# Pooled attention and a tanh-shrink MLP on one core: loads ahead of stores, key placement on ScalarE, product seven in halves, values of two blocks a unit later

## The chip, the core and the metric

The kernel runs on one core of a Trainium2 chip. The metric is the device time in microseconds (us) of one execution; lower is better. Five engines work side by side and wait for each other through semaphores: TensorE (PE, with its weight loads shown apart as PEld), VectorE (DVE), ScalarE (ACT), GpSimd (POOL) and SyncE (SP), which here only issues DMAs. Each engine takes its instructions in the order of the program.

## What is computed

The reference, cut to what matters (batch 8, 8 heads, 576 positions, 64 per head; `w_in` is 512 x 2048, `w_out` 2048 x 512):

```python
k_p = k.reshape(B, H, 72, 8, D).mean(axis=3)
v_p = v.reshape(B, H, 72, 8, D).mean(axis=3)
attn = softmax(q @ k_p.T / sqrt(D))          # with the row maximum taken off
x = (attn @ v_p) as 4608 tokens of 512
h = x @ w_in
g = h - tanh(h)
out = g @ w_out
```

## The kernel before

**Groups.** The 4608 tokens are worked in nine groups of 512. Groups 0 to 7 are the first 512 positions of a batch element; group 8 holds the last 64 positions of all eight, the tails. Two batch elements make one tail unit. While group g runs its MLP, the attention of batch element nb = g + 1 is computed between its matmuls, and keys, values and queries of later elements are loaded.

**First half of a group.** `h_mms` (L445) runs 64 matmuls of 512 columns, four for each of 16 slices of the hidden layer. After every second slice `h_act` takes the tanh on ScalarE (L458) and subtracts it on VectorE into `gT` (L459). All 64 read `xT`, so they need all four blocks of the group's `x`.

**Second half, groups 3 to 8 (`SEVEN`).** The product with `w_out` is done as seven products of quarter matrices, with sums of quarters made beforehand. Their order is 4, 2, 7, 1, 6, 5, 3. Each has two column halves b = 0 and 1 of eight matmuls of 256 columns (L591), so there are 14 units u = 0 to 13, called 4b0, 4b1, 2b0 and so on here. Products 4, 7, 1, 6, 5, 3 add into one PSUM bank for each b, and `evacuate` copies the state of the bank out after each (L606, L608, L611 on ScalarE, L618 on VectorE for product 3). `g_sum` (L573) makes the left-hand sums: S3 in two halves (`g_sum(3, 0, 4)` after slice 13 and `g_sum(3, 4, 8)` after slice 15, stored in the memory of `q_raw[1]`), read by product 7; S2, read by product 6; two on GpSimd, read by product 5; and `g_sum(4)`, after unit 8, read by product 3. `finish_11` and `finish_22` on GpSimd complete the two output halves, and `store_half` stores each (512 KB).

**Attention between the matmuls.** Four blocks of 128 rows, and a tail unit when the element closes a pair (nb = 5 and 7 among these groups). For each: scores on PE (`s`, L311; reads `qT` and `KB`), row maximum and subtraction on VectorE (L323, L326), exp on ScalarE into E (`e`, L362), a DMA transpose of E into ET (`t`, L371), values on PE (`a`, L398), normalisation on VectorE (L419, L420), and a DMA transpose of x into `xT` (`x`, L428). `PLAN7` says at which slice (negative numbers) or after which unit each step stands. Its second half before the change:

```python
0: [("e", 3), ("t", 1)],
3: [("a", 0, P67)],
5: [("a", 1, P45), ("x", 0)],
6: [("a", 2, P67)],
7: [("a", 3, P45), ("x", 1)],
9: [("sb", 4, P45)],
11: [("e", 4), ("t", 2)],
```

P45 and P67 are pairs of PSUM banks. The values and the x transpose of a tail unit are carried into the next group (`carry`, after units 9 and 10).

**Keys, values, queries.** `pool_k` (L214, L217, L220) and `pool_v` (L229 to L256) pool on GpSimd. The pooled keys `kd` are transposed by DMA into `kT` (`k_turn_dma`, L272), and `k_place_kT` (L266) copies them by two instructions of 64 partitions x 288 into `KB`, before on GpSimd. Queries are cast on ScalarE (L280) and transposed by DMA (`q_turn_dma`, L286). Tail queries are loaded (`tail_pieces`, L176), cast on GpSimd (`tail_cast`, L184) and transposed by DMA (`turn_tail`, L187).

**SP's queue.** SP issues every DMA of groups 3 to 6, one after the other in program order, and waits at an entry whose data aren't ready. Before the change, the second half of a group that has later elements to load (groups 3 to 5) issues in this order: values of element nb + 1; transpose of E (blocks 2 and 3, unit 0); transpose of q; first transpose of x (unit 5); second transpose of x, then of kT, then the tail loads when nb is even (unit 7); transpose of the tail's E (unit 11, when there is a tail); store of half 1 (unit 11); keys and queries of a later element (`load_for`, unit 13); store of half 0 (unit 13).

Of the kernel before, what the change touches and what calls it, by code (L numbers as in the profile page):

```python
# [31 lines left out]
NQ = NHID // 2  # L32
HC = DM // 2
SEVEN = (3, 4, 5, 6, 7, 8)
# [4 lines left out]
def kernel(  # L39
# [83 lines left out]
    def raw_of(b):  # L123
        return 1 if b == 1 else 0
# [30 lines left out]
    def k_pieces(b):  # L155
        return row_pieces(k_rows, k_raw, b)
# [13 lines left out]
    def run(pieces, n=16):  # L170
        for _ in range(min(n, len(pieces))):
            pieces.pop(0)()

    def tail_pieces(i, eng=None):
        return [
            lambda s=s: (eng or nc.sync).dma_start(  # L176
                out=tl_raw[64 * s : 64 * s + 64, :, :],
                in_=q[2 * i + s, :, QA:S, :].rearrange("h p d -> p h d"),
            )
            for s in range(2)  # L180
        ]

    def tail_cast(i):
        nc.gpsimd.tensor_copy(out=tl_bf[i % 2][:, :, :], in_=tl_raw[:, :, :])  # L184
# [25 lines left out]
    def pool_k(b, eng, t0=0, t1=NT):  # L210
        r = k_raw[raw_of(b)].rearrange("p t (j d) -> p t j d", d=D)[:, t0:t1, :, :]
        kd = kds[b % 2][:, t0:t1, :, :]
        n = t1 - t0
        eng.tensor_tensor(  # L214
            out=r[:, :, 0:4, :], in0=r[:, :, 0:4, :], in1=r[:, :, 4:8, :], op=ALU.add
        )
        eng.tensor_tensor(  # L217
            out=r[:, :, 0:2, :], in0=r[:, :, 0:2, :], in1=r[:, :, 2:4, :], op=ALU.add
        )
        return eng.tensor_tensor(  # L220
            out=kd,
            in0=r[:, :, 0:1, :].to_broadcast([128, n, 2, D]),
            in1=r[:, :, 1:2, :].to_broadcast([128, n, 2, D]),
            op=ALU.add,
        )
# [50 lines left out]
    def k_place_kT(b, eng):  # L276
        k_place(b, kTs[b % 2].rearrange("p t c -> p (t c)")[:, 0:NK], (eng, eng))
# [297 lines left out]
    XB, YB = 2, (0, 1)  # L575
    PRODUCTS = ("4", "2", "7", "1", "6", "5", "3")

    def product(n, b):

        A, a0, B_ = {  # L580
            "1": (gT[:, HI, C1], 0, w2b[:, HI, C1]),
            "2": (gT[:, LO, C1], 0, w2b[:, LO, C1]),
            "3": (gT[:, LO, C1], 0, w2b[:, LO, C2]),
            "4": (gT[:, LO, C2], 0, T4),
            "5": (gT[:, HI, C2], 0, T1),
            "6": (S2, 0, T2),
            "7": (S3, 0, T3),
        }[n]
        ps = PS[:, XB, HC * b : HC * b + HC] if n == "2" else PS[:, YB[b], 0:HC]
        for i in range(NQ):  # L590
            nc.tensor.matmul(  # L591
                ps,
                lhsT=A[:, i, 128 * b : 128 * b + 128],
                rhs=B_[:, i, :],
                start=(n in "24" and i == 0),
                stop=(i == NQ - 1),
                skip_group_check=True,
            )

    def evacuate(n, b, plain=False):  # L600
        ps = PS[:, YB[b], 0:HC]
        if n == "2":
            if b == 1:
                nc.scalar.copy(out=p2, in_=PS[:, XB, :].rearrange("p (b c) -> p b c", b=2))
        elif n in "47":
            nc.scalar.copy(out={"4": n0, "7": n1}[n][:, b, :], in_=ps)  # L606
        elif n == "6":
            nc.scalar.copy(out=o_hs[1][:, b, C1], in_=ps)  # L608
        elif plain and n in "15":
            dst = o_hs[0][:, b, C1] if n == "1" else o_hs[1][:, b, C2]  # L610
            nc.scalar.copy(out=dst, in_=ps)  # L611
        else:
            dst, sub = {
                "1": (o_hs[0][:, b, C1], n1),
                "5": (o_hs[1][:, b, C2], n0),
                "3": (o_hs[0][:, b, C2], n1),
            }[n]
            nc.vector.tensor_sub(out=dst, in0=ps, in1=sub[:, b, :])  # L618
# [7 lines left out]
    def finish_22(eng):  # L626
        o = o_hs[1][:, :, C2]
        eng.tensor_tensor(out=o, in0=o, in1=n0, op=ALU.subtract)

    def store_half(g, hf):  # L630
        blk = out[g * S : g * S + QA, :].rearrange("(p j) m -> p j m", j=R)
        nc.sync.dma_start(out=blk[:, 2 * hf : 2 * hf + 2, :], in_=o_hs[hf][:, :, :])
# [18 lines left out]
    ve, se, ge = nc.vector.tensor_copy, nc.scalar.copy, nc.gpsimd.tensor_copy  # L651
# [167 lines left out]
    def load_for(g):  # L819


        r = []
        if g + 2 < B:
            if g in SEVEN:
                r += k_pieces(g + 2) + q_pieces(g + 2)
            else:
                r += (v_pieces(g + 1) if g == 2 else []) + q_pieces(g + 2) + k_pieces(g + 2)
        run(r)
# [28 lines left out]
    for u in range(16):  # L857
# [50 lines left out]
    P23, P45, P67 = (2, 3), (4, 5), (6, 7)  # L908
# [8 lines left out]
        0: [("e", 3), ("t", 1)],  # L917
        3: [("a", 0, P67)],
        5: [("a", 1, P45), ("x", 0)],
        6: [("a", 2, P67)],  # L920
        7: [("a", 3, P45), ("x", 1)],
        9: [("sb", 4, P45)],
        11: [("e", 4), ("t", 2)],
    }
    late, carry = [], []

    def tail_values(i):
        av_mms(slot_tl, av_tail(i), P67)
# [6 lines left out]
    for g in range(1, NG):  # L935
        nb = g + 1 if g + 1 < B else None
        more = nb is not None and nb + 1 < B

        tail = {2: 0, 3: 1, 5: 2, 7: 3}.get(nb)
# [33 lines left out]
            pool_v(nb, nc.gpsimd)  # L973
        if more and g in SEVEN:
            pool_k(nb + 1, nc.gpsimd)
        shs = {}

        def seven_more(u):
            if u == 0:
                q_turn_dma(nb + 1)  # L980
            if u == 7:
                k_turn_dma(nb + 1)
                if nb % 2 == 0:
                    run(tail_pieces(nb // 2))
            if u == 13:
                k_place_kT(nb + 1, ge)
                if nb % 2 == 0:
                    tail_cast(nb // 2)
                load_for(g + 1)

        def step(kind, n, bk=None):
            if kind == "t2":
                e_turn_dma(units[2][2], n, n + 1)
                return
            if kind == "t":
                e_turn_dma(units[2 * n][2], 0, 2 if n < 2 else 1)
                if tail and n == 0:
                    turn_tail(tail)
                return
            if kind == "x":  # L1000
                x_turn_dma(xs[n], *((nb, 2 * n, 2) if n < 2 else (B, tail, 1)))
                return
            s, a, sl = units[n]
            if kind == "s" and bk:
                s_mms(s, bk)
                ng = s_max(bk)
                late.append(lambda: s_exp_heads(bk, ng, sl))
            elif kind in ("s", "sb"):
                bk = bk or PAIRS[s_pairs[n]]
                s_mms(s, bk)  # L1010
                shs[n] = s_shift(bk)
            elif kind == "e":
                s_exp(shs[n], sl)
            else:
                bk = bk or PAIRS[a_pairs[n]]
                av_mms(sl, a, bk)
                normalise(bk, xs[n // 2][:, n % 2, :, :, :])
# [23 lines left out]
            run(v_next)  # L1041
        for u in range(14 if g in SEVEN else 0):
            n, b = PRODUCTS[u // 2], u % 2
            product(n, b)
            evacuate(n, b, nb is not None)
            for it in plan.get(u, ()):
                step(*it)
                run_late()
            if nb is not None and u in (9, 10) and carry:
                carry.pop(0)()  # L1050
            if more:
                seven_more(u)
            if nb is not None and u == 2:
                dep = g_sum(2, 0, NQ)
                after([g_sum(1, 0, 4, nc.gpsimd), g_sum(1, 4, NQ, nc.gpsimd)], dep)
            if u == (3 if nb is None else 8):
                g_sum(4, 0, NQ)
            if g == NG - 1:
                if n == "1" and b:
                    finish_11(nc.vector)  # L1060
                    store_part(0, C1, 0, 2)
                elif n == "6" and b:
                    store_part(1, C1, 0, 2)
                elif n == "5" and b:
                    store_part(1, C2, 0, 2, (nc.sync, nc.scalar))
                elif n == "3":
                    store_part(0, C2, b, b + 1, (nc.sync, nc.scalar))
            elif b:
                if n == "1":
                    finish_11(nc.gpsimd, nb is not None)  # L1070
                elif n in "53":
                    if n == "5" and nb is not None:
                        finish_22(nc.gpsimd)
                    store_half(g, 0 if n == "3" else 1)
        if g in SEVEN and tail is not None:
            carry += [lambda i=tail: tail_values(i), lambda i=tail: x_turn_dma(x_tl, B, i, 1)]
        for u, (tb, qd) in enumerate(() if g in SEVEN else UNITS):
# [53 lines left out]
```

## Time and profile before

| what | value |
|---|---|
| median of 3 runs | 295.48 us (294.96 to 295.68) |
| the profiled execution | 294.32 us |
| its span, first to last instruction | 292.6 us |
| TensorE clock granted | 1.0 |
| TensorE busy | 280.9 us (96%) |
| VectorE busy | 222.0 us (76%) |
| GpSimd busy | 153.0 us (52%) |
| ScalarE busy | 147.4 us (50%) |
| largest TensorE groups | h_mms 100.8 us, products and o_mms 44.7 + 35.0 us |

Times in the profile are microseconds from the start of the span. The profile page gives busy time by engine, queues and groups of instructions; other views of the same trace list who waited for whom, the instructions in order of time, and busy time in chosen windows. In a list in order of time the columns are start, length, engine, line, operation, out<-in, shapes and count; merged instructions stand on one line. A DMA's length there is its issue on the queue; its landing comes later.

### The profile page before, as it was taken

What the parts mean: (1) busy time and instruction counts of PE and PEld (TensorE: products, weight loads), DVE (VectorE), ACT (ScalarE), POOL (GpSimd) and SP (SyncE); (2) the same over time, 40 slices, a digit from 0 to 9 for tenths busy, and PEclk for the clock granted to TensorE, in tenths of its full rate; (3) what the DMA queues carried; (4) which work ended last, traced back from release to release, by engine and by line L of the source; (5) the groups of instructions that cost most, each with busy time, mean ns of one, the idle gap of its engine ahead of it and who ended that gap; (6) DMA issues with size and microseconds to landing.
All of it is one profiled execution on the core that took longest, in us unless ns stands there. A gap on an engine that the chain in (4) does not pass through costs nothing.

```text
span 292.6 us, 5473 instructions
## 1 busy us (share of the span) xinstructions
PE 280.9 (96%) x2154; PEld 179.0 (61%) x2163; DVE 222.0 (76%) x310; ACT 147.4 (50%) x220; POOL 153.0 (52%) x126
## 2 busy tenths in 40 slices
PE   7799999999999999999999899989999999999994
PEld 2489955444544455458845784478547854884583
DVE  6786876988848976699579976996599847935782
ACT  2786752466326831576257634773375336415630
POOL 7839871448512960982979589729840920010000
PEclk9999999999999999999999999999999999999999
DMA  7999999799999998887889968969623641011005
GB/s 229 228 285 273 205 275 219 151 307 299 228 230 275 299 245 197 278 224 209 146 237 265 258 145 249 281 197 165 197 43 62 78 166 21 0 72 76 0 2 143
DMA packets 84474, 54.56 MB, mean 186 GB/s; under 512 B 59904, under 2 KB 73344, under 8 KB 84448
## 3 DMA queue, kind: packets, MB, share of 16 engines
q1 hardware_dynamic: 77744, 45.17, 62.5%
q0 software_dynamic: 6320, 8.65, 14.1%
q10 hardware_dynamic: 384, 0.39, 0.5%
q8 instruction: 17, 0.28, 0.4%
q14 instruction: 9, 0.07, 0.1%
HBM read 36.70 MB, written 9.44 MB: 158 GB/s over the span
## 4 chain that ended last, share of the span: by engine, by line
PE 69%; DVE 20%; ACT 5%; DMA 3%; issue 1%; ACTq 0%; DVEq 0%
PE PS L445 24%; PE PS L591 20%; PE PS L513 14%; DVE gT L459 10%; PE PS L465 4%; PE PS L398 4%; DVE sh L326 3%; DVE mx L323 3%; PE PS L311 2%; ACT t_sb L458 2%; DMA ET<-E 2%; DVE q_raw L573 2%; DMA k_raw<-in_k_dram 1%; PE PS L292 1%; ACT ET L381 1%
## 5 line engine op out<-in xcount | busy, mean ns | idle before, releaser
L445 PE MATMUL PS<-xT,w1b 128*128 128x512 bf16 x448 | 100.8, 379 | 0.0
L459 DVE TENSOR_TENSOR gT<-PS,t_sb 128x1024 bf16<-128x1024 f32 x64 | 76.8, 1217 | 27.4 <-ACT t_sb L458 27.2
L458 ACT ACTIVATE t_sb<-PS 128x1024 f32<-128x1024 f32 x64 | 65.5, 1024 | 54.4 <-PE PS L445 53.0
L445 PEld LDWEIGHTS <-w1b 128*128 128x128 bf16 x512 | 49.4, 98 | 55.2 <-issue 0.3
L591 PEld LDWEIGHTS <-gT 128*128 128x128 bf16 x480 | 46.0, 98 | 5.8
L513 PE MATMUL PS<-w2b,gT 128*128 128x512 bf16 x183 | 44.7, 379 | 0.5
L591 PE MATMUL PS<-w2b,gT 128*128 128x256 bf16 x288 | 35.0, 272 | 0.0
L573 POOL TENSOR_TENSOR gT<-gT 128x1024 bf16<-128x1024 bf16 x8 | 16.8, 2119 | 25.9 <-DVE rden L419 25.9
L513 PEld LDWEIGHTS <-gT 128*128 128x128 bf16 x192 | 17.4, 98 | 17.4
L323 DVE TENSOR_REDUCE mx<-PS 128x8 f32<-128x576 f32 x35 | 26.1, 747 | 1.7 <-PE PS L311 1.7
L326 DVE TENSOR_TENSOR sh<-PS,mx 128x576 f32<-128x576 f32 x35 | 26.5, 757 | 1.2
L362 ACT ACTIVATE E<-sh 128x576 bf16<-128x576 f32 x31 | 21.1, 682 | 9.5 <-DVE sh L326 9.5
L420 DVE TENSOR_TENSOR x_sb<-PS,rden 128x512 bf16<-128x512 f32 x32 | 22.1, 691 | 1.1
L229 POOL TENSOR_TENSOR v_raw<-v_raw 128x1280 f32<-128x1280 f32 x6 | 17.4, 2893 | 7.5 <-DMA v_raw<-in_v_dram 7.3
L214 POOL TENSOR_TENSOR k_raw<-k_raw 128x1280 f32<-128x1280 f32 x6 | 17.4, 2901 | 6.3 <-DMA k_raw<-in_k_dram 5.5
L618 DVE TENSOR_TENSOR o_h<-PS,q_raw 128x256 f32<-128x256 f32 x20 | 8.5, 424 | 14.7 <-PE PS L591 12.5
L624 POOL TENSOR_TENSOR o_h<-o_h,k_raw 128x512 f32<-128x512 f32 x5 | 7.2, 1440 | 22.2 <-DVE o_h L618 21.9
L419 DVE RECIPROCAL rden<-PS 128x8 f32<-128x8 f32 x36 | 7.3, 203 | 12.9 <-PE PS L398 12.8
L398 PE MATMUL PS<-VB,ET 128*128 128x130 bf16 (+2 forms) x192 | 16.3, 221 | 0.8 <-DMA ET<-E 0.7
L535 ACT COPY o_h<-PS 128x512 f32<-128x512 f32 x10 | 5.7, 582 | 21.1 <-PE PS L513 21.1
L465 PE MATMUL PS<-xT,w1b 128*128 128x128 bf16 x256 | 15.6, 219 | 0.3 <-ACT xT L437 0.3
L398 PEld LDWEIGHTS <-ET 128*128 128x128 bf16 x192 | 13.3, 98 | 4.1 <-DMA ET<-E 1.1
(103 smaller groups left out, 372.0 us busy)
## 6 DMA issues: line engine op xcount, KB each, us to landing
k_raw<-in_k_dram SPq DMA_DIRECT2D x14, 512.0 KB, 7.3
q_raw<-in_q_dram SPq DMA_DIRECT2D x12, 512.0 KB, 7.4
v_raw<-in_v_dram SPq DMA_DIRECT2D x12, 512.0 KB, 5.0
out_dram<-o_h SPq DMA_DIRECT2D x10, 512.0 KB, 3.6
out_dram<-o_h SPq DMA_DIRECT2D x12, 256.0 KB, 2.9
w1b<-in_moe_w_in_dram POOLq DMA_DIRECT2D x4, 512.0 KB, 10.4
q_raw<-in_q_dram POOLq DMA_DIRECT2D x2, 1024.0 KB, 16.4
w2b<-in_moe_w_out_dram POOLq DMA_DIRECT2D x4, 512.0 KB, 11.4
```

Source lines behind the costliest of these rows:

```text
L323: nc.vector.reduce_max(out=mx.rearrange("p k h o -> p k (h o)"), in_=sc, axis=AX.X)
L326: nc.vector.tensor_tensor(out=sh[:, :, :, :], in0=sc, in1=mx.to_broadcast([128, 2, 4, G]), op=ALU.subtract)
L362: nc.scalar.activation(out=E[:, e, :, :].rearrange("p t c -> p (t c)")[:, 0:NK], in_=sh.rearrange("p k h c -> p (k h c)"), func=ACT.Exp, s ...
L398: nc.tensor.matmul(PS[ps, banks[half], D1 * h : D1 * (h + s1 - s0)], lhsT=ET[:, t, c0 : c0 + (ps.stop - ps.start)], rhs=VB[kb][:, t, s0:s1 ...
L420: nc.vector.tensor_tensor(out=x_sb, in0=ps[:, :, :, 0:D], in1=rden.to_broadcast([128, 2, 4, D]), op=ALU.mult,)
L445: nc.tensor.matmul(PS[:, bank, :].rearrange("p (j c) -> p j c", j=R), lhsT=w1b[:, fb, i * 128 : (i + 1) * 128], rhs=xT_of(g)[:, :, fb, :], ...
L458: nc.scalar.activation(out=t_sb[:, :, :], in_=ps, func=ACT.Tanh)
L459: nc.vector.tensor_sub(out=gT[:, i : i + 2, :], in0=ps, in1=t_sb[:, :, :])
L465: mm = nc.tensor.matmul(PS[:, bank, 128 * n : 128 * n + 128], lhsT=w1b[:, fb, (4 * c + n) * 128 : (4 * c + n + 1) * 128], rhs=xT_of(0)[:, ...
L513: mm = nc.tensor.matmul(PS[:, bank, 0 : c1 - c0], lhsT=gT[:, i, tb * 128 : (tb + 1) * 128], rhs=w2b[:, i, c0:c1], start=(i == 0), stop=(i ...
L573: return eng.tensor_tensor(out=o, in0=x, in1=y, op=op)
L591: nc.tensor.matmul(ps, lhsT=A[:, i, 128 * b : 128 * b + 128], rhs=B_[:, i, :], start=(n in "24" and i == 0), stop=(i == NQ - 1), skip_grou ...
```

## The change

- Product 7 of groups 3 to 6 is run as first halves of its contraction for both column halves, then second halves for both; both evacuations follow.
- Values of blocks 2 and 3 (and the second transpose of x) move one unit later, to units 7 and 8. The tail's scores use banks P67 instead of P45.
- Keys are placed by ScalarE instead of GpSimd.
- In groups 3 to 5 the store of half 1 is held until the loads of unit 13 are issued. The tail loads move from unit 7 to behind the store of half 0.
- The cast of the tail queries moves from unit 13 into the next group, behind its `pool_v` and `pool_k`; their transpose moves from the first to the second transpose of E.

```diff
-    def product(n, b):
+    def product(n, b, i0=0, i1=NQ):
...
-        for i in range(NQ):
+        for i in range(i0, i1):
...
-        6: [("a", 2, P67)],
-        7: [("a", 3, P45), ("x", 1)],
-        9: [("sb", 4, P45)],
+        7: [("a", 2, P67)],
+        8: [("a", 3, P45), ("x", 1)],
+        9: [("sb", 4, P67)],
...
-    late, carry = [], []
+    late, carry, held = [], [], []
...
             pool_k(nb + 1, nc.gpsimd)
+        if nb in (5, 7):
+            tail_cast(tail)
...
             if u == 7:
                 k_turn_dma(nb + 1)
-                if nb % 2 == 0:
-                    run(tail_pieces(nb // 2))
             if u == 13:
-                k_place_kT(nb + 1, ge)
-                if nb % 2 == 0:
-                    tail_cast(nb // 2)
+                k_place_kT(nb + 1, se)
                 load_for(g + 1)
+                while held:
+                    held.pop(0)()
...
-                if tail and n == 0:
+                if tail and n == (1 if g in SEVEN else 0):
                     turn_tail(tail)
...
             n, b = PRODUCTS[u // 2], u % 2
-            product(n, b)
-            evacuate(n, b, nb is not None)
+            if n == "7" and nb is not None:
+
+                for t in range(2):
+                    product(n, t, 4 * b, 4 * b + 4)
+                for t in range(2 * b):
+                    evacuate(n, t, True)
+            else:
+                product(n, b)
+                evacuate(n, b, nb is not None)
...
+                    if more and n == "5":
+
+                        held.append(lambda g=g: store_half(g, 1))
+                        continue
                     store_half(g, 0 if n == "3" else 1)
+                    if n == "3" and more and nb % 2 == 0:
+                        run(tail_pieces(nb // 2))
```

## The prediction, made before the change was run

> **What bounds the kernel now.** I read the page first, then busy time by group in windows, then PE's waits, then the timelines around each wait. In this text +x means x us after a group's first h_mms; "7b0" is product seven, column half 0.
>
> ```profile
> PE 280.9 (96%) x2154; PEld 179.0 (61%) x2163; DVE 222.0 (76%) x310; ACT 147.4 (50%) x220; POOL 153.0 (52%) x126
> ```
> ```profile
> core 0: us, PE busy (x) PEld busy (x) DVE busy (x) ACT busy (x) POOL busy (x), PEclk, DMA share, GB/s
> 116.49:145.29 28.80, 28.69 (x217) 19.47 (x216) 22.49 (x29) 16.91 (x26) 21.82 (x14) 1.00 0.86 221
> 145.29:175.66 30.37, 29.43 (x226) 19.67 (x224) 24.91 (x32) 16.91 (x26) 24.38 (x16) 1.00 0.96 222
> 175.66:205.84 30.18, 29.40 (x231) 19.97 (x229) 24.44 (x32) 16.36 (x25) 22.76 (x15) 1.00 0.89 221
> 205.84:235.16 29.32, 29.12 (x227) 19.76 (x225) 24.39 (x32) 15.35 (x24) 17.09 (x13) 1.00 0.44 90
> ```
>
> The four windows are groups 3, 4, 5 and 6. PE is the bound at full clock, so the change can only win PE's own stalls. I measure them start to start: a 256-column matmul follows the last after 0.109 us where nothing waits.
>
> ```profile
> PEld L591 <- DVE q_raw L573: 2.4, 4, 1.1
> ...
> PEld L398 <- DMA ET<-E: 1.1, 2, 1.0
> ```
> ```profile
> 194.32 0.60 PE L591 MATMUL PS<-v_raw,q_raw 128*128 128x256 bf16 x4
> 195.71 1.48 PE L591 MATMUL PS<-v_raw,q_raw 128*128 128x256 bf16 x12 [0.78 <-DVE q_raw L573]
> ```
>
> First wait: in each group 7b0 runs four matmuls and stops for the second half of S3 (q_raw, L573). Group 5: 194.32 + 4 x 0.109 = 194.76, resumed at 195.71: 0.95. By the same reading group 3 loses 0.28 (135.15, 135.87), group 4 0.40 (164.09, 164.92), group 6 0.36 (224.50, 225.29). Second wait: in group 4 the values of block 2 stand behind 1b0 (166.60 + 0.87 = 167.47) and begin at 168.34: 0.86. Third: group 4's first scores follow KB, which GpSimd finished at 147.97, 0.13 late. Sum 0.28 + 0.40 + 0.95 + 0.36 + 0.86 + 0.13 = 2.98 us.
>
> Why group 5 is the worst:
>
> ```profile
> 191.06 1.27 DVE L573 TENSOR_TENSOR q_raw<-gT 128x1024 bf16<-128x1024 bf16 x1
> ```
> ```profile
> 185.62 2.91 POOL L214 TENSOR_TENSOR k_raw<-k_raw 128x1280 f32<-128x1280 f32 x1 [1.54 <-DMA k_raw<-in_k_dram]
> ...
> 190.23 1.55 POOL L220 TENSOR_TENSOR kd<-k_raw 128x640 bf16<-128x640 f32 x1
> ```
>
> S3's first half takes 1.27 instead of 0.69: GpSimd's last key sum runs beside it, late because its load was. That is 0.58 of the 0.95.
>
> Why group 4's values wait:
>
> ```profile
> GB/s 355 383 437 396 314 382 437 437 314 355 424 437 224 236 200 210 203 104 14 0 0 3 9 9 10 10 12 271 288 292 285 272 290 288 292 283 278 265 237 236
> ...
> q8 instruction: 1, 0.02, 1.4%
> ...
> ET<-E SPq DMA_TRANSPOSE x1, 4.5
> ```
> ```profile
> 163.75 1.51 SPq L371 DMA_TRANSPOSE ET<-E  x1
> 165.31 3.64 SPq L286 DMA_TRANSPOSE qT<-q_bf  x1
> 169.05 3.27 SPq L428 DMA_TRANSPOSE xT<-x_sb  x2
> 172.42 1.23 SPq L272 DMA_TRANSPOSE kT<-kd  x1
> ```
>
> In 163 to 169 us one q8 packet (1.4% of 16 engines x 6 us = 1.3 us) holds a DMA engine; about then traffic falls to nothing for 1.3 us (slices of 0.15), and the transpose of E lands after 4.5 us; the three undisturbed ones (groups 3, 5, 6) took 3.5 to 3.6.
>
> **The change, part by part.**
>
> *Product seven by halves.* The same 16 matmuls, but eight (0.87 us) instead of four (0.44) precede the wait: up to 0.436 won in each group: 0.28 + 0.40 + 0.436 + 0.36 = 1.48. Both evacuations now follow 7b1. 1b0 overwrites the first's bank; between them lie 7b1's second half (0.44) and the values of block 1 (0.36), against a 0.37 copy (L606): hidden; without that cover, some 0.4 a group.
>
> *Loads ahead of stores.* Group 3's five key and query loads were issued at 146.97 to 150.20, behind two tail loads and a store that waits for GpSimd's finish_22; now they follow the transposes, near 143. Group 4's stay behind the transpose of El, but lose the 0.5 MB store ahead. I put its keys' landing at 6.8 to 7.4 us after the first issue (6.8 with small stores in front, issued 117.88, landed 124.65; 8.5 now), so +8.1 to +8.8, and the last key sum ends at +14.3 to +15.0 (9.96 to 16.12 now), before S3's first half at +15.4. I take the whole 0.58, of which the halves leave 0.51 to win; bound below: 0. Moved late: store 1 goes past five issues (3.2 us), the tail loads past both stores. Their next users (o_hs at about +20, tl_bf at +18) hide that.
>
> *Keys by ScalarE.* 2 x 0.42 leave GpSimd; on ScalarE 2 x 0.40 (its copies take 0.37 at 256 columns, 0.58 at 512). Queued behind them is the next group's first tanh, which waits for PE until +2.0. kT, issued now before the second x transpose, lands at -2 to -0.3; the copies end by +0.5, or +1.3 behind El's exp. Hidden, and the 0.13 is won; each us of kT beyond that would delay the tanh.
>
> *Tail cast and its transpose.* The cast (0.61) moves behind pool_v and pool_k and ends near 160.5; behind it GpSimd does nothing until 166.3. Its transpose (1.24 SP issue) moves from ahead of the v loads, which gain 1.3, to behind the second transpose of E: ahead of q's, both x's and kT's. This weighs in group 4 alone (group 6 has no q or k to turn).
>
> *Values of blocks 2 and 3 a unit later.* Block 2's gain 0.87 on E's transpose; in groups 3, 5, 6 it landed 0.05 to 0.26 before them, so without this the won stall would return there. Block 3's cost: from their last matmul to the x transpose 1.17 (140.02 to 141.19), 2.73 to landing (141.22, 143.95) = 3.90. Left before the next group: 5 x 0.872 = 4.36, plus tail work 0.38 in groups 4 and 6, 0.65 in group 5. Spare 0.46, 0.84, 1.11, 0.84 where it was 1.3 or more. g_sum(4), now behind the later normalise, ends 0.1 before product three in group 3: I charge 0.05, at worst 0.3 (group 4's took 1.79 instead of 1.39 beside GpSimd).
>
> *Group 4.* The q8 packets are PE's code: 17 of them for 4317 PE and PEld instructions, one per 254, and q8's rate follows PE's. That count hardly moves at product seven, so by its nearest row E lands at 168.3 again. Its reader now is a unit later: (175.66 - 168.34) - 0.87 = 6.45 us remain, next group at 174.79, gain 0.87 of 1.26. The x transpose: traffic resumes at 167.05 with some 6.7 us of blocks queued (1.0 of E, 0.55 of the tail, 2.3 of q, 1.15, 0.7 and 1.0 of x, k and x, by size from q's 2.3 us for 16 blocks) and lands near 174.4. Simply adding the SP times gives 175.5, gain 0.1. I take 0.87, the traffic being what bounds there.
>
> The Trainium skill, page "Runtime: NRT & Kernel Launch", section "Instruction fetch mechanics", says that each engine streams its code in 16 KiB blocks and that crossing a block is mostly hidden. By that, this fetch would cost nothing, group 4 would gain its full 1.26, and the sum would be 2.93; the row disagrees here.
>
> Sum: 0.28 + 0.13 + 0.87 + (0.436 + 0.51) + 0.36 - 0.05 = 2.54 us. The profiled execution is 294.32 (span 292.6 and 1.7 around): 291.8 there. The median of the runs is 295.48, 1.16 above it: 292.9. Bounds: high 2.98; low 0.28 + 0.13 + 0.1 + 0.44 + 0.36 - 0.3 = 1.0.
>
> **Rivals.**
> 1. *The code fetch misses E's transpose* (PE's order around product seven changes, so it may fall earlier). Gain 2.93, 292.5. This is the time that the page's rule gives too. For: the count is the same only to some ten instructions. Against: the fetch fell just as PE was released at 164.9, which stays.
> 2. *Half of it does not come.* The keys still land late (group 5 keeps 0.51) and group 4's queue of transposes eats its gain: 1.0, so 294.5. For: SP's list there is tight. Against: the store ahead is gone.
> 3. *Slower: the second x transpose becomes the wait at the start of groups 4 to 7.* Its place is SP's queue behind kT. Transposes at L428 took 2.7 to 4.7 us to land (median 3.0). At 4.7 everywhere it is late by 1.51 + 1.13 + 0.86 + 1.13 = 4.6 us, against 2.54 won: 297.6. It decides from about 4.2 us in all four. For: loads now follow directly behind it, and spare is 0.46 in group 3. Against: a transpose with loads right behind (116.60, landed 119.51) took 2.9, and 4.7 needs a fetch in each group.
> 4. *Late in two of the groups:* about 2.2 lost, no change, 295.2.
>
> **How the numbers follow.** Forecast 292.9: 0.58. Rival 1: 0.13. Rival 2: 0.13, a quarter of it within the bound. Rival 3: 0.10. Rival 4: 0.06. A measurement here tells about 0.3% (0.9 us) from no change. Faster 0.58 + 0.13 + 0.10 = 0.81; same 0.06 + 0.03 = 0.09; slower 0.10. The range runs from rival 1 less 0.4 of run scatter (292.1) to rival 2 (294.6).
>
> **What would show it.** Right: PE's wait on L573 gone in groups 3, 4, 6 and below 0.1 in group 5; S3's halves at 0.7; KB groups on ACT with no PE wait behind; groups 3 to 6 at about 28.5, 29.4, 29.2 and 29.0 us. Wrong: PE waiting on xT at a group's start, on gT before product three, or ScalarE's tanh waiting on kT.

## The result, and the profile after

The changed kernel takes 293.63 us (median of 6 runs, 293.31 to 294.31) against 295.58 for the kernel before (6 runs on the same chip, 294.68 to 296.13). The ratio is 0.9942, 95% interval 0.9923 to 0.9961: faster by 1.1 to 2.3 us. The forecast was 2.54 us less, 292.9.

Page of the changed kernel, its first lines; then busy time by engine in the windows of groups 3 to 6, cut as before at each group's first h_mms:

```profile
span 291.6 us, 5474 instructions
...
PE 280.5 (96%) x2154; PEld 179.2 (61%) x2163; DVE 223.5 (77%) x310; ACT 150.1 (51%) x226; POOL 149.7 (51%) x120
```
```profile
117.09:146.14 29.05, 28.64 (x217) 19.54 (x216) 23.18 (x29) 17.66 (x28) 22.13 (x14) 1.00 0.89 225
146.14:175.81 29.67, 29.28 (x226) 19.75 (x224) 25.29 (x33) 17.31 (x27) 22.89 (x15) 1.00 0.81 222
175.81:205.03 29.22, 29.22 (x228) 20.09 (x228) 24.21 (x32) 17.75 (x29) 21.40 (x12) 1.00 0.92 223
205.03:234.16 29.13, 29.13 (x227) 19.75 (x224) 25.02 (x32) 15.20 (x24) 16.29 (x11) 1.00 0.45 96
```

The first number behind a window is its length. Groups 3 to 6 together fell from 118.67 to 117.07, by 1.60 us. The stretch ahead of group 1, which is not changed, was 0.60 longer in this execution (it ends at 54.16 against 53.56), which is why the span shows only 1.0. Group 5 won all of its 0.96. But group 3 got longer, 28.80 to 29.05, and groups 4 and 6 won less than was there.

The old waits are gone: no wait for S3 or for ET is left in these groups. In PE's lists two others stand in their place:

```profile
PEld L591 <- DVE gT L573: 1.2, 3, 0.7
```
```profile
PE PS L445 <- DMA xT<-x_sb: 0.7, 2, 0.4
```

The first is product three waiting for g_sum(4): start to start 0.57, 0.15, 0 and 0.17 us in groups 3 to 6. The second is the start of group 5, which waits 0.56 us start to start for `xT` (the other of the two waits on that line is ahead of group 1, at 54.16). Here is the first in group 3, from the lists in order of time of GpSimd, VectorE and PE:

```profile
141.98 1.27 POOL L623 TENSOR_TENSOR o_h<-o_h,q_raw 128x512 f32<-128x512 f32 x1
143.33 2.12 POOL L624 TENSOR_TENSOR o_h<-o_h,k_raw 128x512 f32<-128x512 f32 x1
```
```profile
142.24 2.09 DVE L573 TENSOR_TENSOR gT<-gT,S 128x2048 bf16<-128x2048 bf16 x1
```
```profile
144.38 1.81 PE L591 MATMUL PS<-w2b,gT 128*128 128x256 bf16 x15 [0.41 <-ACT o_h L611]
```

g_sum(4) takes 2.09 instead of 1.39. It starts 0.26 behind the first sum of finish_11 (L623). That sum ends at 143.25, and 1.1 later so does g_sum(4); finish_11's second sum (L624), begun in the middle, takes 2.12 instead of 1.27 and ends 1.12 behind g_sum(4). By these times each stands still while the other runs. Before the change g_sum(4) began at 141.10, while GpSimd's last sum for product five was still running (to 141.41), and got in ahead of finish_11, whose first sum then took the longer time:

```profile
141.10 1.39 DVE L573 TENSOR_TENSOR gT<-gT,S 128x2048 bf16<-128x2048 bf16 x1
```
```profile
141.37 2.25 POOL L623 TENSOR_TENSOR o_h<-o_h,q_raw 128x512 f32<-128x512 f32 x1
```

The 0.41 that the PE line puts down to ScalarE's copy L611 is the list's guess: that copy of this bank had ended at 143.5, g_sum(4) at 144.33.

And the second in group 4, from SP's and PE's lists:

```profile
169.85 1.76 SPq L428 DMA_TRANSPOSE xT<-x_sb  x1
171.66 1.27 SPq L272 DMA_TRANSPOSE kT<-kd  x1
173.02 1.26 SPq L428 DMA_TRANSPOSE xT<-x_sb  x1
```
```profile
175.81 1.46 PE L445 MATMUL PS<-xT,w1b 128*128 128x512 bf16 x6 [0.40 <-DMA xT<-x_sb]
```

Block 3 was normalised at 171.37, but SP issued its transpose at 173.02, behind kT; it landed at 175.77 and the group began at 175.81.

### The profile page after: what moved, and what is told of

It reads as the page before. It is cut to its first block, busy times and chain, and to the rows that moved or that the text cites. A ratio compares the mean times of both kernels' runs of the same rounds, so it can differ in the third digit from the quotient of the medians.

```text
span 291.6 us, 5474 instructions
## 1 busy us (share of the span) xinstructions
PE 280.5 (96%) x2154; PEld 179.2 (61%) x2163; DVE 223.5 (77%) x310; ACT 150.1 (51%) x226; POOL 149.7 (51%) x120
## 4 chain that ended last, share of the span: by engine, by line
PE 86%; DMA 4%; ACT 4%; DVE 3%; issue 1%; SPq 0%; ACTq 0%
PE PS L445 37%; PE PS L591 24%; PE PS L513 12%; PE PS L398 5%; PE PS L465 4%; PE PS L311 3%; DMA q_raw<-in_q_dram 2%; DMA xT<-x_sb 2%; PE PS L292 1%; ACT qT L700 1%; DVE x_sb L420 1%; ACT ET L381 1%; ACT E L346 1%; DVE gT L573 1%; DVE gT L459 0%
## 5 line engine op out<-in xcount | busy, mean ns | idle before, releaser
L591 PE MATMUL PS<-w2b,gT 128*128 128x256 bf16 x288 | 34.4, 273 | 0.4 <-ACT o_h L611 0.4
L573 POOL TENSOR_TENSOR gT<-gT 128x1024 bf16<-128x1024 bf16 x8 | 16.8, 2120 | 30.6 <-DVE rden L419 30.6
L624 POOL TENSOR_TENSOR o_h<-o_h,k_raw 128x512 f32<-128x512 f32 x5 | 9.8, 1956 | 22.2 <-DVE o_h L618 21.8
```

The costliest lines, as they stand in the source:

```text
L573: return eng.tensor_tensor(out=o, in0=x, in1=y, op=op)
L591: nc.tensor.matmul(ps, lhsT=A[:, i, 128 * b : 128 * b + 128], rhs=B_[:, i, :], start=(n in "24" and i == 0), stop=(i == NQ - 1), skip_grou ...
```

## The experiments

All are made from the changed kernel unless it says otherwise. A time has its ratio to the kernel before, run on the same chip, with the 95% interval. The times of one kernel scatter by 1 to 3 us there (the kernel before by up to 4.3), so what tells small effects apart is the length of groups 3 to 6 in the profiled execution, one of each kernel, cut as above; where a group had no wait it came out alike within 0.02 us in all kernels (28.46 to 28.47, 28.94 to 28.95, 29.21 to 29.22, 28.95 to 28.96).

| kernel | median us, ratio | groups 3, 4, 5, 6 | sum |
|---|---|---|---|
| before | | 28.80, 30.37, 30.18, 29.32 | 118.67 |
| changed | 293.63, 0.9942 (0.9923 to 0.9961) | 29.05, 29.67, 29.22, 29.13 | 117.07 |
| finish_11 behind g_sum(4) | 294.0, 0.9956 (0.9940 to 0.9973) | 28.47, 30.26, 29.21, 28.95 | 116.89 |
| kT behind x | 294.57, 0.9968 (0.9946 to 0.9990) | 29.04, 30.02, 29.22, 29.13 | 117.41 |
| both | 292.92, 0.9925 (0.9898 to 0.9952) | 28.46, 29.83, 29.22, 28.95 | 116.46 |
| values back | 293.93, 0.9952 (0.9930 to 0.9973) | 28.82, 30.03, 29.45, 29.06 | 117.36 |
| both, kT behind x in group 4 only | 292.15, 0.9876 (0.9843 to 0.9909) | 28.47, 29.17, 29.22, 28.95 | 115.81 |
| the same, cast behind S3 | 291.74, 0.9875 (0.9851 to 0.9900) | 28.46, 28.95, 29.22, 28.95 | 115.58 |
| before with halves alone | 294.78, 0.9975 (0.9955 to 0.9995) | 28.79, 30.83, 30.17, 29.08 | 118.87 |
| stores first | 293.13, 0.9912 (0.9883 to 0.9940) | 29.05, 29.41, 29.47, 29.13 | 117.06 |
| keys on GpSimd | 293.53, 0.9928 (0.9899 to 0.9956) | 29.05, 29.80, 29.21, 29.13 | 117.19 |
| block 3 at unit 7 | 292.65, 0.9895 (0.9865 to 0.9924) | 28.46, 30.08, 29.22, 28.95 | 116.71 |
| block 3 at unit 7, kT by group | 291.91, 0.9885 (0.9859 to 0.9911) | 28.47, 28.94, 29.22, 28.96 | 115.59 |

### finish_11 behind g_sum(4)

```diff
             if u == (3 if nb is None else 8):
-                g_sum(4, 0, NQ)
+                dep4 = g_sum(4, 0, NQ)
+                if nb is not None:
+                    after(finish_11(nc.gpsimd, True), dep4)
```

> The changed kernel with one edit: in groups 3 to 6 GpSimd's two finish_11 sums are issued behind VectorE's g_sum(4) and wait for it. Theory: in the changed kernel g_sum(4) takes 2.1 us instead of 1.22 because a GpSimd sum from SBUF is running when it starts (142.24 against 141.98 in group 3) and the two cannot run together, and product three waits 0.57, 0.15, 0 and 0.17 us in groups 3 to 6. Then here g_sum(4) takes 1.22 in every group, PE's wait before product three is gone, group 4 still starts its successor late on xT (it gives its 0.15 back there), and the time falls by about 0.74 to 292.9. Rival: product three waits for ScalarE's copy of product five's bank (the list of PE's waits names ACT o_h L611 once, 0.4 us); then the wait stays and the time is 293.6.

Measured: every g_sum(4) takes 1.22 us (all instances of L573 on `S`):

```profile
L573 DVE TENSOR_TENSOR gT<-gT,S x6: 1215/1216/1218, 143.6 to 281.6; 128x2048 bf16<-128x2048 bf16 x6
```

No wait before product three is left, and groups 3 and 6 fall by 0.58 and 0.18. The rival (ScalarE's copy) falls: that copy was not touched. Group 4 grew by 0.59, more than expected: it waited 1.05 on `xT`, where SP's issues stood 0.6 us later in the group than in the changed kernel, and 0.23 at product seven, where the tail cast (162.18 to 162.78) met S3's first half (162.32, 1.00 instead of 0.68).

### kT behind the second x transpose

```diff
-            if u == 7:
+            if u == 8:
                 k_turn_dma(nb + 1)
```

> The changed kernel with one edit: the transpose of kT is issued after unit 8, behind the second transpose of x, instead of after unit 7, ahead of it. Theory: in group 4 the x transpose was ready at 171.37 (end of the normalisation) and was issued at 173.02 because SP was busy with kT and what stands before it; PE waits 0.56 us for xT at the start of group 5. Here it is issued 1.3 us earlier, that wait is gone and the time is about 293.1. Keys land 1.3 us later and ScalarE's copies end about 0.9 us before the tanh behind them. Rival: the blocks on the DMA engines, not SP's order, set when x lands; then x lands at the same time, group 5 still waits 0.5 us, and the time is 293.6.

Measured: the wait on `xT` is gone, so SP's order was its cause; the transfer itself took as long as before from issue to landing (2.77 us, 2.75 in the changed kernel). But group 4 lost 0.33 + 0.12 at its first scores and 0.33 at product seven. ScalarE's list at its start:

```profile
148.62 0.88 ACT L266 COPY KB<-kT 64x288 bf16<-64x288 bf16 x2 [3.74 <-DMA kT<-kd]
149.53 1.02 ACT L458 ACTIVATE t_sb<-PS 128x1024 f32<-128x1024 f32 x1
```

kT of group 3, issued at 144.18, landed only at 148.54: a q8 packet of 1.04 us began at 146.44, in the middle of it. The key copies stood in front of the first tanh, which began 2.9 us into the group instead of 2.0. What was expected for this ("0.9 us before the tanh") was wrong by that packet.

### Both

> Both edits: finish_11 behind g_sum(4) and kT behind the second transpose of x. Theory: both waits are gone, 0.57 + 0.15 + 0.17 + 0.56 = 1.45 us less than the changed kernel, about 292.2; groups 3 to 6 take 28.5, 29.0, 29.2 and 29.0 us in the trace. Rivals as for the two alone: 293.6 if neither wait has that cause; or about 292.9 if, with product three earlier by 0.6 us in group 3, the x transpose (landing 0.5 us ahead of its need there) becomes the next wait.

Measured: the two gains add in groups 3 and 6 and on `xT`, and the same loss as in the last kernel stays in group 4 (0.38 + 0.12 + 0.33).

### Values of blocks 2 and 3 back at units 6 and 7

```diff
-        7: [("a", 2, P67)],
-        8: [("a", 3, P45), ("x", 1)],
+        6: [("a", 2, P67)],
+        7: [("a", 3, P45), ("x", 1)],
```

> The changed kernel with the values of blocks 2 and 3 and the second x transpose back at units 6 and 7. Theory: what the later unit gives and costs is close to even. Given back: block 2's values stand 0.87 us earlier and meet E's transpose, 0.26 us in group 3, 0.3 in group 4, 0.2 in group 5 and 0.1 in group 6 (E landed at 138.99, 168.04, 197.63 and 226.75; they would begin at 138.73, 167.78, 197.45, 226.67). Won: g_sum(4) and the x transpose come earlier, so up to 0.57 + 0.15 + 0.17 before product three and 0.56 on xT. Sum: 0.86 against 1.45, about 293.0. The rival is the prediction's reading, that the later unit is needed and costs 0.05: then this is slower, about 294.4.

Measured: 117.36, 0.29 longer than the changed kernel, where 0.6 less was expected. Both new waits (1.45 us) are gone, but E's transpose is met early in all four groups, by 0.34, 0.59, 0.22 and 0.10 (1.25 us); group 4's:

```profile
169.98 0.53 PE L398 MATMUL PS<-VB,ET 128*128 128x130 bf16 x6 [0.43 <-DMA ET<-E]
```

Group 4 lost 0.43 more at its scores and at product seven. That loss comes from another order that this edit changed too: the second x transpose, at unit 7 again, goes out ahead of kT. So kT of group 3 was issued at 144.51, a q8 packet of 1.19 us began at 146.59, kT landed at 148.83, and the first tanh behind the key copies began 2.5 us into the group instead of 2.0, as in "kT behind x". Without that, the earlier units would come out about even with the later ones, as expected (1.25 against 1.45). So this run does not show that the later unit pays for both blocks; "block 3 at unit 7" below takes the two apart.

### kT behind x in group 4 only

The two edits of "both", with the unit chosen by `tail`:

```diff
-            if u == 7:
+            if u == (7 if tail is None else 8):
                 k_turn_dma(nb + 1)
```

> The changed kernel with finish_11 behind g_sum(4), and kT behind the second x transpose only in groups with a tail unit (group 4 among those that load keys); in groups 3 and 5 it stays ahead. Theory: with kT behind x everywhere, group 4 lost 0.50 us at its first scores, because the keys landed late and ScalarE's copies of them held the first tanh, and 0.33 more at product seven, because VectorE's chain started late by that; here kT of group 3 is early again and both go. Groups 3 to 6 take 28.5, 29.0 to 29.25, 29.2 and 28.95 us; the 0.25 in group 4 is product seven's wait if GpSimd's tail cast, later by 1.3 us, meets S3's first half. About 0.6 us less than with both edits everywhere, 1.2 to 1.4 less than the changed kernel. Rival: the 0.50 comes from something else in that run's start; then group 4 stays at 29.8.

Measured: the 0.50 is gone. 0.22 us is left in group 4, at product seven; GpSimd's and VectorE's lists there:

```profile
161.24 0.61 POOL L184 CAST tl_bf<-tl_raw 128x512 bf16<-128x512 f32 x1
```
```profile
161.41 0.99 DVE L573 TENSOR_TENSOR q_raw<-gT 128x1024 bf16<-128x1024 bf16 x1
```

### The cast behind S3's first half

The last kernel, and in groups 4 and 6 the tail cast no longer at the head of the group:

```diff
-                        g_sum(n, i0, i0 + 4)
+                        dep3 = g_sum(n, i0, i0 + 4)
+                        if i0 == 0 and nb in (5, 7):
+                            after([tail_cast(tail)], dep3)
```

> The changed kernel with finish_11 behind g_sum(4), kT behind x in group 4 only, and the tail cast on GpSimd behind S3's first half. Theory: the one wait left is 0.22 us at product seven in group 4: S3's first half took 0.99 us instead of 0.69 because the cast (161.24 to 161.85) was running on GpSimd when it began (161.41). Here the cast waits, S3's first half takes 0.69, that wait goes and group 4 takes 28.95. The time is 0.2 us below the version without the wait for the cast. Rival: the last key sum, which ends at 161.29, is what it met; then 0.1 to 0.2 us of the wait stay.

Measured as expected: S3's halves take 0.68 to 0.69 in every group and group 4 takes 28.95. This is the second pair of VectorE and GpSimd instructions that was set apart and stopped slowing.

### Halves alone, on the kernel before

The edits to `product` and to its call, nothing else of the change.

> The kernel before with product seven by halves and nothing else. Theory: the waits for S3's second half fall from 0.28, 0.40, 0.95 and 0.36 us to 0, 0, 0.5 and 0, but the values of block 2 then meet E's transpose 0.23 us early in group 3, wholly in group 4 (nothing won there: the same landing sets it), 0.2 in group 5 and 0.1 in group 6. Net 0.05 + 0 + 0.24 + 0.26 = 0.55 us of 1.48, about 294.7 to 294.9. Rival: the transposes come earlier with PE, as everything else does, and 1.48 are won.

Measured: over ten executions the time is 0.25% lower (0.05 to 0.45%, 0.1 to 1.3 us), in line with what was expected. In the profiled execution, which at 295.38 was among the slower of them, nothing is won (118.87 against 118.67). There E takes back 0.32 in group 3 for the 0.28 won. In group 4 S3's first half met the last key sum, which had begun 0.34 earlier:

```profile
161.26 1.54 POOL L220 TENSOR_TENSOR kd<-k_raw 128x640 bf16<-128x640 f32 x1
```
```profile
161.60 1.76 DVE L573 TENSOR_TENSOR q_raw<-gT 128x1024 bf16<-128x1024 bf16 x1
```

That made VectorE late for the scores of block 3 too, whose bank the values of block 0 need (0.45), and for S3 (0.45 left of more), and E took 0.87. Only group 6 won, 0.24. The rival (1.48 won) falls, if narrowly by the times of the runs; alone, the halves give less than was there to win.

### Stores first

```diff
-                    if more and n == "5":
-
-                        held.append(lambda g=g: store_half(g, 1))
-                        continue
                     store_half(g, 0 if n == "3" else 1)
```

> The changed kernel with the store of half 1 not held, so that it stands again ahead of the key and query loads and waits for GpSimd there (the tail loads stay behind the stores). Theory: the loads of group 3 start 3 us later (near 146.8), those of group 4 land 1.5 to 2 us later, GpSimd's key sums end beside S3's first half, and product seven waits about 0.3 us in group 4 and 0.5 in group 5: 0.8 slower than the changed kernel. Rival: GpSimd's own queue (value sums first), not the load, sets when the key sums run; then groups 4 and 5 take 29.7 and 29.2 us as in the changed kernel.

Measured: no difference in the sum, 117.06. Group 4 has no wait for S3: its key sums end at 160.28, as GpSimd's value sums ahead of them, not the load, set most of their time (the load cost 0.60). So there the rival is right. In group 5 the theory is, at half its size: the last key sum (189.40 to 190.95) meets S3's first half, 1.00 instead of 0.68, and product seven waits 0.25. That 0.25 is what the loads ahead of stores are worth here. In these two kernels and in the kernel before, group 5's first key sum begins 0.16 us behind the landing of the last key load, which came 9.80 us into the group before, 9.52 here and 8.86 in the changed kernel. The 0.25 doesn't show in the sum because group 4 waited 0.29 for `xT` instead of 0.56, E's second transpose having been issued in 1.73 instead of 2.01 us.

### 40 more warm-up matmuls, on the kernel before

```diff
     fill(11, 7)
+    fill(40, 7, 64)
```

> The kernel before with 40 more warm-up matmuls of 64 columns at its start: the computation is the same, and every q8 packet comes 80 PE instructions earlier in PE's program. Theory: E's second transpose of group 4 was late because a q8 packet fell on it. Shifted by 40 matmuls (4.4 us in the products), that packet falls before it, and in groups 5 and 6 the packets that fell at unit 8 now fall at E's transpose: the wait for ET moves from group 4 (0.86 us) to groups 5 and 6 (0.5 to 1 us each), where E's transpose now takes 4.3 us or more to land. Rival: in group 4 E waited for the value loads ahead of it on the queue (last landing 167.24); then the wait stays in group 4 and groups 5 and 6 have none. The start may be longer by up to 3 us.

Measured, one execution, 295.03 us, groups 28.79, 30.41, 29.72, 29.33: half right. Group 4's packet came at 160.63, its E took 3.51 us to land instead of 4.54, and no wait for ET was left there. (E's issue and PE's arrival both came 0.9 us later in the group than before: S3's first half had met the last key sum there and taken 1.78, and product seven waited 0.98.) In group 5 a packet began 0.43 us behind E's issue and E took 3.78 to land, 0.3 longer, with a wait of 0.12 instead of the 0.5 to 1 expected; in group 6 one began 0.66 before E landed, E took 3.65, 0.2 longer, and PE did not wait. So the packets do move with PE's program, and without one E landed in time. The rival as it was put falls, since the wait did not stay; but the value loads ahead of E came earlier too: the last one landed 1.70 us behind E's issue here and 3.49 before. Whether the packet held E itself, or those loads on the DMA engine that it took, no run separates.

### Keys on GpSimd

```diff
-                k_place_kT(nb + 1, se)
+                k_place_kT(nb + 1, ge)
```

> The changed kernel with the keys placed by GpSimd again. Theory: ScalarE's placing is worth little by itself: GpSimd's copies end near +1.4 in groups 4 and 5, ahead of the first scores at +2.6, and what follows on GpSimd is 0.9 us later, so the tail cast meets S3's first half in group 4 (0.3 us at product seven), which the 0.56 wait on xT there takes up. Same time as the changed kernel within 0.3 us. Rival: GpSimd's load was what made S3 late; then groups 4 and 5 lose 0.5 us each.

Measured: 117.19, within 0.12 of the changed kernel. The expected meeting of the cast and S3 did not come about. ScalarE's placing is worth 0.1 us at most; the 0.13 at group 4's first scores stayed won without it, since kT is issued ahead of x (it landed 2.90 us after its issue at 140.76; in the kernel before, a q8 packet at 144.68 fell into it and it took 4.47).

### Block 3 at unit 7

```diff
-        7: [("a", 2, P67)],
-        8: [("a", 3, P45), ("x", 1)],
+        7: [("a", 2, P67), ("a", 3, P45), ("x", 1)],
```

> The changed kernel with the values of block 3 and the second x transpose at unit 7, directly behind those of block 2, and nothing else. Theory: only block 2 had to move. E's transpose is met as late as in the changed kernel, so no wait there. Block 3's normalisation ends 0.4 us earlier than in the changed kernel (VectorE does block 2's first), so g_sum(4) asks for the port 0.1 to 0.2 us before GpSimd's second g_sum(1) ends and goes ahead of finish_11: 1.2 to 1.4 us long and no wait before product three. The second x transpose stands ahead of kT: no wait on xT in group 4. Groups 3 to 6: 28.5, 29.1, 29.2, 28.95, about 1.3 us less than the changed kernel. Rival: finish_11 still gets in first, g_sum(4) stays at 2.1 us and product three waits 0.5 us in some groups.

Measured: both new waits are gone by this alone, g_sum(4) takes 1.25 to 1.40 us in groups 3 to 6 and no GpSimd sum had to be held: it asks 0.2 to 0.3 us before GpSimd's second g_sum(1) ends. But kT now stands behind x in every group, and group 4 paid 0.64 + 0.12 + 0.33, as in "kT behind x": kT of group 3 was issued at 143.65, a q8 packet of 1.73 us began at 144.91, it landed at 148.12.

```profile
148.20 0.88 ACT L266 COPY KB<-kT 64x288 bf16<-64x288 bf16 x2 [3.47 <-DMA kT<-kd]
```

### Block 3 at unit 7, kT by group

The last edit, and `u == (6 if tail is None else 7)` for `k_turn_dma`.

> The changed kernel with two edits: values of block 3 and the second x transpose at unit 7, and the transpose of kT after unit 6 (ahead of that x transpose) in groups without a tail, after unit 7 (behind it) in group 4. Theory: with block 3 at unit 7 alone, group 4 lost 0.64 + 0.12 us at its first scores and 0.33 at product seven because kT of group 3, issued behind the x transpose, was hit by a q8 packet (144.91, 1.73 us long), landed near 148.1 and held ScalarE's key copies and so its first tanh. Here kT of group 3 is out 1.3 us or more earlier, ahead of that packet, and all three go. Groups 3 to 6: 28.5, 29.0, 29.2, 28.95; the same time as the version with finish_11 behind g_sum(4) and the cast behind S3 (291.7), without any added wait. Rival: the packet, not the order, is the cause, and comes earlier too; then group 4 stays near 30.

Measured as expected, in all four groups. The packet still came (144.60, 1.63 us), but kT had landed at 143.98. Busy time in the windows of groups 3 to 6:

```profile
117.16:145.63 28.47, 28.47 (x218) 19.65 (x217) 22.24 (x29) 17.66 (x28) 21.56 (x14) 1.00 0.92 231
145.63:174.57 28.94, 28.94 (x226) 19.80 (x224) 24.17 (x32) 17.02 (x26) 22.86 (x15) 1.00 0.85 229
174.57:203.79 29.22, 29.22 (x230) 20.09 (x228) 23.57 (x32) 18.05 (x29) 22.18 (x13) 1.00 0.93 228
203.79:232.75 28.96, 28.96 (x227) 19.83 (x225) 24.18 (x32) 15.46 (x24) 16.24 (x11) 1.00 0.44 92
```

PE is busy from end to end of all four windows. This version and the one with the cast behind S3 beat both kernels, by the same 3.1 us in these groups against the kernel before; this one does it with two edits of the plan and no added wait. Their intervals overlap, so the runs do not tell them apart.

## Why the prediction was right, and what was mis-sized

The bound and the waits were read rightly: 2.98 us of PE's own stalls stood in groups 3 to 6, and 2.98 - 0.89 - 0.56 = 1.53 of 1.60 are accounted for by the waits that went and the two that came. Against the forecast, two waits cost more than it charged, and one that it charged did not come. Point by point:

- *Product seven by halves:* no wait for S3 in groups 3, 4 and 6, as forecast (1.04 us). Alone it made the time 0.1 to 1.3 us lower over ten executions, and won nothing in the profiled one (halves alone).
- *Group 5:* all 0.95 won, S3's halves at 0.68 and 0.69. The keys landed 7.77 us after the first issue, not 6.8 to 7.4, and the last key sum ended at +15.20 instead of +14.3 to +15.0, only 0.21 ahead of S3's first half. The reason given, loads ahead of stores, accounts for 0.25 of the win (stores first). The rest of the 0.51 that I gave to the loads came without them: behind the same store, the last key load landed 7.55 us after the first issue there, against 8.48 before, and GpSimd's key sums follow that landing. Why the loads were quicker is not settled.
- *Keys by ScalarE:* the 0.13 was won, but by kT's earlier issue, not by ScalarE. The hiding that I named did hold here; the rival price, a tanh held by a late kT, is real and was paid in four experiments.
- *E's second transpose in group 4:* 0.86 won, and the 0.39 that I left for a repeated code fetch was not lost: the packet began 0.41 us behind E's issue instead of 1.20, and E landed after 3.59 (168.04) with its reader at 168.65. This was my first rival's mechanism, so here the forecast was too low, and that hid part of the two misses below. I had held that the packet stays; it came 0.94 us earlier in the group (18.72 against 19.66). The value loads ahead of E were earlier as well (the last landed 0.51 us behind E's issue, 3.49 before), and no run separates the two.
- *The step that failed first: "I charge 0.05, at worst 0.3" for product three.* It measured 0.57 + 0.15 + 0 + 0.17 = 0.89. I had the slow instance (1.79) before me and took it for an upper end. With block 3 a unit later, g_sum(4) asks 0.2 to 0.3 us after GpSimd has begun finish_11, and must wait out that sum: about 0.9 on top of 1.22. The sum should have been made by who asks first, in each group.
- *The second: group 4's x transpose, charged 0 beyond E.* It cost 0.56. I had worked out both figures, 174.4 by traffic and 175.5 by adding SP's times, which are 29.1 and 30.2 us behind the group's first h_mms, and took the traffic. It landed between them, at 29.6 (175.77 - 146.14). It was SP that held it: the issue came 1.65 us behind block 3's normalisation, with kT ahead of it, and with kT behind it the wait went. The lower bound of the sum held this case.
- *The slower rival:* its wait came in one group of four. The 0.56 at the start of group 5 is that wait; spare was enough in groups 3, 5 and 6.

So the sign and the main terms held, two small charges, 0.05 and 0, were 0.89 and 0.56, and the 0.39 did not come: 2.54 - 0.84 - 0.56 + 0.39 = 1.53 of the 1.60 measured in these groups. The first is the Trainium skill's lock, page "SBUF — State Buffer", section "Who interferes with whom": a VectorE instruction with two SBUF inputs contends with a GpSimd instruction that reads SBUF, the lock is exclusive, and issue order decides who blocks. The traces agree: waiting time and own time add up to within 0.15 us (2.12 and 2.09 where alone 1.27 and 1.22).

## What to carry to other kernels

When a step is moved later, list what runs on the other engine that shares its port at the new time, and ask who asks first: a sum that used to slip in ahead can land behind one a whole instruction long. On an in-order DMA queue, add up the issue times between a transfer's data and its place in the queue, and put the one that the next stage needs first, group by group. And before a copy that waits for a DMA is put on an engine with slack, look at what stands behind it there: it cost nothing while the DMA was early and 0.4 to 1.1 us when one packet hit it.

## What the runs showed of the hardware that was not expected

- VectorE's sums of two SBUF operands and GpSimd's instructions hold each other up: 1.22 became 2.1, 0.69 became 1.0 to 1.8. Who asks first decides. Asking 0.2 to 0.3 us after GpSimd had begun finish_11 cost 0.9 us; asking 0.2 to 0.3 us before GpSimd's running sum ended let g_sum(4) in ahead of the next one, at 1.25 to 1.40 (block 3 at unit 7).
- The q8 packets are PE's code: 80 more PE instructions at the start brought group 4's from 19.7 to 13.9 us into the group. Each is 16 KB and holds a DMA engine for 0.9 to 2.2 us. Where one fell into kT's transpose, in seven of these kernels (once in each), kT took 3.7 to 4.5 us to land, and 2.6 to 3.2 where none did. E's second transpose in group 4 took 4.54 with a packet 1.2 us behind its issue, 3.4 to 4.1 with one 0.3 to 0.8 behind it, and 3.5 with none.
